# Issuing all engines' instructions straight into the main program instead of into a block with branches and a closing barrier

## The chip, the cores and the metric

The kernel runs on one core of a Trainium2 chip. The profile has records of five engines: TensorE (PE; busy for 246.9 of the 251.6 us of the kernel before), VectorE (DVE; 215.9), ScalarE (ACT; 114.6), GpSimd (POOL; 32.6) and SyncE (SP), whose records are transfers, waits and its share of two barriers, with one branch; none of them counts as busy time. The metric is the device time of one execution in microseconds (us); lower is better. Every run also has a *span*: from the start of the program's first instruction to the end of its last. Time minus span is called "the remainder" below: the part of the measured time that lies outside the program's own instructions. Spans are on record to 0.1 us, so one remainder is good to some 0.05 us. The remainder also holds whatever lies before the first instruction.

## The reference

One layer on 2048 tokens of 640 features in bfloat16. It is cut here to what matters; the change doesn't touch the arithmetic.

```python
x  = A_x                                   # 1 x 2048 x 640
xn = layernorm(x)
q, k, v = split(xn @ wqkv)                 # 32 heads of 20
# each token looks at itself and at 7 earlier ones, 2 apart
o  = softmax(q . k[window] * 20 ** -0.5) @ v[window]
g, u = xn @ w_gate, xn @ w_up              # 1536 features each
return x + o @ wo + (g * u) @ w_down
```

## The kernel before

A small scheduler records every operation with its dependences, and then writes one list of instructions and waits per engine. This is how the lists become a program:

```python
    def emit(self, finals):
        ...                                   # (cut: which waits each instruction needs)
        for X in finals:                      # finals: the nine stores of the output
            prog["sp"].append((0,) + X.event)
        clock = self.clock

        def make_section(ename):
            def section(eng):
                for it in prog[ename]:
                    if it[0] == 0:
                        eng.wait_ge(it[1], it[2])
                        continue
                    ...                       # (cut: issue the instruction, attach its semaphore)
            return section

        with nc.Block() as block:
            block.sync(make_section("sp"))
            block.scalar(make_section("act"))
            block.tensor(make_section("pe"))
            block.vector(make_section("dve"))
            block.gpsimd(make_section("pool"))
```

The block gives each engine a piece of program of its own: a branch into it at the start, a branch out of it at the end (ten as written; the trace has only one of them, see step 2 at the end), and then a barrier of all five engines (in the trace of before five DRAINs and six semaphore instructions at L208, of which the last ends at 251.55 us). An opening barrier, ahead of the block, belongs to the main program and is there with or without the block (it releases the engines from some 0.66 us on). SyncE's list ends with waits for the stores.

The last token tile is stored in three parts; in the profile of before the last matmul ends at 249.26 us by the trace, and the last store, of 32 KB, is issued at 249.62:

```python
            if last:
                eng = "act" if c0 == DHALF else "sp"
                stores.append(dma(ohbm[t * TS:(t + 1) * TS, cols], o, r=[o], name=f"odma{t}_{c0}", eng=eng))
```

Of the kernel before, what the change touches and what calls it, by code (L numbers as in the profile page):

```python
# [41 lines left out]
class Sched:  # L42
# [115 lines left out]
    def emit(self, finals):  # L158
        nc = self.nc
        counters = {e: 0 for e in ENGINES}  # L160
        for X in self.ops:
            if not X.dma and X.needs_tick:
                counters[X.eng] += 1
                X.event = (self.clock[X.eng], counters[X.eng])
        know = {e: {} for e in ENGINES}
        prog = {e: [] for e in ENGINES}
        for X in self.ops:
            E = X.eng
            kn = know[E]
            needed = {}  # L170
            for d in X.deps:
                sem, val = d.event
                if kn.get(sem, 0) >= val:
                    continue
                cur = needed.get(sem)
                if cur is None or cur[0] < val:
                    needed[sem] = (val, d)
            for sem, (val, d) in sorted(needed.items(), key=lambda t: -t[1][1].idx):
                if kn.get(sem, 0) >= val:
                    continue  # L180
                prog[E].append((0, sem, val))
                for s2, v2 in d.pre_know.items():
                    if kn.get(s2, 0) < v2:
                        kn[s2] = v2
                kn[sem] = max(kn.get(sem, 0), val)
            X.pre_know = dict(kn)
            prog[E].append((1, X))
        for X in finals:
# [9 lines that stand above are left out]
                    X = it[1]  # L198
                    ins = X.fn(eng)
                    if ins is not None and X.name:  # L200
                        ins.annotate(X.name)
                    if X.dma:
                        ins.then_inc(X.event[0], 16)
                    elif X.needs_tick:
                        ins.then_inc(clock[ename], 1)
            return section

        with nc.Block() as block:  # L208
            block.sync(make_section("sp"))
            block.scalar(make_section("act"))  # L210
            block.tensor(make_section("pe"))
            block.vector(make_section("dve"))
            block.gpsimd(make_section("pool"))


def build_kernel(nc, A_x, A_wqkv, A_wo, B_x, B_w_gate, B_w_up, B_w_down, out):
# [773 lines left out]
```

## Time and profile before

| What | Before |
|---|---|
| median of the first three runs | 253.53 us (253.51 to 253.69) |
| profiled run: time, span, remainder | 253.35, 251.6, 1.75 us |
| TensorE busy | 246.9 us, 98% of the span |
| first recorded 512-wide matmul of the back-to-back stretch starts | 18.21 us |
| last store is issued | 249.62 us |
| from there to the end of the span | 1.93 us |

The prediction shows the page's lines and the instructions of the closing barrier. This one is the timeline of TensorE of the kernel before, where the long back-to-back stretch begins; columns: start in us, duration in us, engine, line, operation, output and inputs.

```profile
18.21 0.38 PE L479 MATMUL PS<-XNT,WQKV 128*128 128x512 bf16 x1
```

From here to 249.30 us TensorE is busy for 230.05 of 231.09 us, and the chain that ended last holds nothing but its matmuls over that stretch, with gaps of at most 0.05 us: there the time is that of the matmuls. Ahead of it stands the start of the kernel, where loads and layer norms alternate.

### The profile page before, as it was taken

Reading aid. Unit: us, or ns where it says so; the run is one execution under the profiler, and the core shown is the slowest. Engines: PE = TensorE matmul, PEld = TensorE weight load, DVE = VectorE, ACT = ScalarE, POOL = GpSimd, SP = SyncE. Lnnn points to the kernel's source line nnn. Section 1 sums busy time; section 2 is a strip of 40 time slices with the busy share of each in tenths; the row PEclk is TensorE's granted clock in tenths of the full one; section 3 lists DMA queues with packets and bytes.
Section 4 is the critical chain, followed back from the end, with each engine's and each line's share of the span. In section 5 each row is a group of like instructions: output and inputs, shape, how many; then the busy total and the mean of one; then the engine's idle time right before and its main releaser. Section 6 shows DMA issues by size and latency. Waiting matters only on the chain.

```text
span 251.6 us, 3257 instructions
## 1 busy us (share of the span) xinstructions
PE 246.9 (98%) x1274; PEld 128.9 (51%) x1294; DVE 215.9 (86%) x255; ACT 114.6 (46%) x203; POOL 32.6 (13%) x41
## 2 busy tenths in 40 slices
PE   8999999999999999999999999999999999999996
PEld 3995555555544444444444444444444444445775
DVE  4899889999999953999999994899999999995221
ACT  5486657555555557555555553225555011111000
POOL 1000001044434231002331100002000000200200
PEclk9999999999999999999999999999999999999999
DMA  6999879674678462355369932296500011581651
GB/s 181 318 268 211 111 211 406 153 123 87 126 146 136 75 125 42 143 195 104 63 128 269 491 111 42 42 337 57 89 0 3 21 42 21 78 112 23 95 136 52
DMA packets 33775, 33.78 MB, mean 134 GB/s; under 512 B 17984, under 2 KB 30272, under 8 KB 33728
## 3 DMA queue, kind: packets, MB, share of 16 engines
q1 hardware_dynamic: 27280, 24.13, 33.6%
q0 software_dynamic: 6192, 9.31, 22.7%
q8 instruction: 10, 0.16, 0.3%
q10 hardware_dynamic: 288, 0.13, 0.2%
q14 instruction: 5, 0.04, 0.0%
HBM read 14.42 MB, written 4.59 MB: 76 GB/s over the span
## 4 chain that ended last, share of the span: by engine, by line
PE 91%; DVE 3%; SPq 2%; DMA 2%; issue 1%; ACT 0%
PE PS L642 41%; PE PS L669 22%; PE PS L479 21%; PE PS L701 7%; SPq L298 2%; DMA XST<-in_A_x_dram 2%; DVE STATS L376 1%; DVE STATS L382 1%; DVE MV L388 0%; DVE XNS L423 0%; ACT SD L389 0%; DVE FOUT L705 0%; DVE SD L408 0%
## 5 line engine op out<-in xcount | busy, mean ns | idle before, releaser
L642 PE MATMUL PS<-XNT,WU 128*128 128x512 bf16 x237 | 59.0, 379 | 0.2
L642 PE MATMUL PS<-XNT,WG 128*128 128x512 bf16 x232 | 57.9, 379 | 0.4
L479 PE MATMUL PS<-XNT,WQKV 128*128 128x512 bf16 x245 | 53.7, 379 | 0.3
L609 DVE TENSOR_TENSOR PVB<-VO,ATB 128x10240 f16<-128x10240 bf16 x8 | 43.9, 5488 | 0.2
L479 PEld LDWEIGHTS PS<-XNT,WQKV 128*128 128x128 bf16 x250 | 29.4, 118 | 24.4
L644 ACT ACTIVATE USX<-PS 128x512 bf16<-128x512 f32 x48 | 28.7, 597 | 22.6 <-PE PS L642 22.6
L642 PEld LDWEIGHTS PS<-XNT,WU 128*128 128x128 bf16 x240 | 23.5, 98 | 28.3
L642 PEld LDWEIGHTS PS<-XNT,WG 128*128 128x128 bf16 x240 | 23.5, 98 | 28.3
L604 DVE TENSOR_TENSOR PVB<-PVB 128x5120 f16<-128x5120 f16 (+1 forms) x16 | 34.5, 2154 | 0.3
L537 POOL DMA_DIRECT2D LOG<-PE x24 | 21.9, 925 | 58.3 <-DMA LOG<-PE 58.3
L644 ACT ACTIVATE HT<-PS 128x512 bf16<-128x512 f32 x36 | 21.5, 597 | 16.4 <-PE PS L642 16.4
L675 ACT ACTIVATE DT<-PS 128x512 f16<-128x512 f32 x15 | 8.9, 596 | 42.6 <-PE PS L669 39.5
L669 PE MATMUL PS<-HT,WD 128*128 128x512 bf16 x118 | 27.4, 379 | 0.1
L526 DVE TENSOR_TENSOR TMP<-QH,KH 128x2048 f16<-128x2048 bf16 x16 | 19.1, 1217 | 1.0 <-ACT KH L486 0.9
L669 PEld LDWEIGHTS PS<-HT,WD 128*128 128x128 bf16 x120 | 11.7, 98 | 14.2
L526 DVE TENSOR_TENSOR PP<-QH,KH 128x2048 f16<-128x2048 bf16 x16 | 18.9, 1217 | 0.0
L531 DVE TENSOR_TENSOR PP<-PP,TMP 128x4096 f16<-128x4096 f16 x8 | 18.3, 2291 | 0.2
L669 PE MATMUL PS<-VO,WO 128*128 128x512 bf16 x74 | 18.4, 379 | 0.0
L705 DVE TENSOR_TENSOR FOUT<-PS,XR 128x320 bf16<-128x320 f32 (+2 forms) x9 | 4.1, 454 | 15.3 <-PE PS L701 15.3
L537 POOL DMA_DIRECT2D PE<-PP x8 | 8.3, 1043 | 63.1 <-DVE PP L532 63.1
L486 ACT ACTIVATE VO<-PS 128x512 bf16<-128x512 f32 x20 | 11.9, 597 | 8.7 <-PE PS L479 8.7
L647 DVE TENSOR_TENSOR HT<-HT,USX 128x512 bf16<-128x512 bf16 x36 | 14.3, 415 | 1.7 <-ACT USX L644 1.7
(71 smaller groups left out, 220.7 us busy)
## 6 DMA issues: line engine op xcount, KB each, us to landing
PE<-PP POOLq DMA_DIRECT2D x8, 512.0 KB, 4.8
ATB<-LOG SPq DMA_DIRECT2D x8, 512.0 KB, 4.9
LOG<-PE POOLq DMA_DIRECT2D x24, 128.0 KB, 2.7
WG<-in_B_w_gate_dram SPq DMA_DIRECT2D x1, 1920.0 KB, 8.0
WU<-in_B_w_up_dram SPq DMA_DIRECT2D x1, 1920.0 KB, 14.6
WD<-in_B_w_down_dram SPq DMA_DIRECT2D x1, 1920.0 KB, 10.0
out_dram<-in_A_x_dram SPq DMA_DIRECT2D x1, 1920.0 KB, 10.5
out_dram<-FACC POOLq DMA_DIRECT2D x3, 640.0 KB, 6.7
```

Of the source, the lines that this page charges most:

```text
L479: op("pe", (lambda l, x, c: lambda e: e.matmul(PS[:, b, :], l, x, start=(c == 0), stop=(c == NCH - 1)))(l, x, c), r=[l, x], w=[PS[:, b, :] ...
L486: op("act", lambda e: e.activation(o, PS[:, b, :], ACT.Copy, scale=sc), r=[PS[:, b, :]], w=[o], name=f"pev{which}_{m}_{j}")
L526: return (1.22, lambda: op("dve", lambda e: e.tensor_tensor(o, qw, kw, ALU.mult), r=[q, k], w=[o], name=f"prod{h}_{p}_{c}"))
L531: (2.3, lambda: op("dve", lambda e: e.tensor_tensor(a, a, b, ALU.add), r=[a, b], w=[a], name=f"psum{h}_{p}")),
L537: op("pool", lambda e: e.dma_start(o, i, accum_op=ALU.add), r=[o, i], w=[o], dma=True, name=name)
L604: return lambda: op("dve", lambda e: e.tensor_tensor(o, x, y, ALU.add), r=[x, y], w=[o], name=f"{name}_{b}")
L609: lambda: op("dve", lambda e: e.tensor_tensor(PVB[:], vw, aw, ALU.mult), r=[v, a], w=[PVB[:]], name=f"pv_{b}")),
L642: op("pe", (lambda l, x, c: lambda e: e.matmul(PS[:, b, :], l, x, start=(c == 0), stop=(c == NCH - 1)))(l, x, c), r=[l, x], w=[PS[:, b, :] ...
L644: op("act", lambda e: e.activation(o, PS[:, b, :], ACT.Copy), r=[PS[:, b, :]], w=[o], name=f"guev{which}_{m}_{j}")
L647: h_pending.append(lambda: op("dve", lambda e: e.tensor_tensor(h, h, o, ALU.mult), r=[h, o], w=[h], name=f"h{m}_{j}"))
L669: op("pe", (lambda l, x, i: lambda e: e.matmul(PS[:, b, :], l, x, start=(i == 0), stop=(i == n - 1)))(l, x, i), r=[l, x], w=[PS[:, b, :]], ...
L701: op("pe", (lambda l, x, i, b, wid: lambda e: e.matmul(PS[:, b, 0:wid], l, x, start=(i == 0), stop=(i == n - 1)))(l, x, i, b, wid), r=[l, ...
```

## The change

The intent: drop what the block adds around the work, which is ten branches and the closing barrier, and let SyncE's waits for the stores be the last thing in the program.

```diff
-        with nc.Block() as block:
-            block.sync(make_section("sp"))
-            block.scalar(make_section("act"))
-            block.tensor(make_section("pe"))
-            block.vector(make_section("dve"))
-            block.gpsimd(make_section("pool"))
+        for ename, eng in (("sp", nc.sync), ("act", nc.scalar), ("pe", nc.tensor), ("dve", nc.vector), ("pool", nc.gpsimd)):
+            make_section(ename)(eng)
```

The file becomes four lines shorter there, so line L298 becomes L294.

## The prediction

> **What bounds the kernel now.** I read the page first: the span, the busy shares, the forty slices and the chain that ended last.
>
> ```profile
> span 251.6 us, 3257 instructions
> PE 246.9 (98%) x1274; PEld 128.9 (51%) x1294; DVE 215.9 (86%) x255; ACT 114.6 (46%) x203; POOL 32.6 (13%) x41
> PE   8999999999999999999999999999999999999996
> ...
> PE 91%; DVE 3%; SPq 2%; DMA 2%; issue 1%; ACT 0%
> ```
>
> TensorE is busy in every slice, at full granted clock, and the chain is TensorE for 91% of the span. The change touches no matmul, load, store or wait between engines in the middle. Compared instruction by instruction, each engine's stream is the same in both programs, in the same order, except at its start and at its end. So two places of the profile matter: the first microsecond and the last two. Next I read the timeline from 248.5 us on:
>
> ```profile
> 248.74 0.35 ACTq L298 DMA_DIRECT2D out_dram<-FOUT  x1
> ...
> 249.30 0.29 DVE L705 TENSOR_TENSOR FOUT<-PS,XR 128x128 bf16<-128x128 f32 x1 [0.59 <-PE PS L701]
> 249.62 0.33 SPq L298 DMA_DIRECT2D out_dram<-FOUT  x1
> ```
>
> The last arithmetic ends at 249.30 + 0.29 = 249.59 us. SyncE then issues the last store, of 32 KB, and the page's list of issues gives such a store 1.5 us to landing: 249.62 + 1.5 = 251.12 us. The rest is the program's ending. I asked for the instructions of the line that opens the block (L208; its closing barrier is put down to it) and of the helper's wait (L196):
>
> ```profile
> L208 POOLq EVENT_SEMAPHORE  x2: 17/17/17, 251.4 to 251.4; - x2
> L208 POOLq DRAIN  x1: 7977/7977/7977, 234.0 to 234.0; - x1
> L208 PEldq DRAIN  x1: 1222/1222/1222, 248.1 to 248.1; - x1
> L208 ACTq DRAIN  x1: 152/152/152, 249.1 to 249.1; - x1
> L208 DVEq DRAIN  x1: 330/330/330, 249.3 to 249.3; - x1
> L208 SPq COMPARE_BRANCH  x1: 41/41/41, 251.2 to 251.2; - x1
> L208 SPq DRAIN  x1: 13/13/13, 251.3 to 251.3; - x1
> L208 SPq EVENT_SEMAPHORE  x1: 17/17/17, 251.5 to 251.5; - x1
> L208 ACTq EVENT_SEMAPHORE  x1: 17/17/17, 251.5 to 251.5; - x1
> L208 DVEq EVENT_SEMAPHORE  x1: 21/21/21, 251.5 to 251.5; - x1
> L208 PEldq EVENT_SEMAPHORE  x1: 51/51/51, 251.5 to 251.5; - x1
> ```
>
> ```profile
> L196 SPq EVENT_SEMAPHORE  x4: 28/28/28, 250.0 to 251.1; - x4
> ```
>
> Columns: line, engine ("q" is its sequencer), operation, count, shortest/median/longest duration in ns, first and last start in us. The reader is to see that the long DRAINs (GpSimd 7977 ns, TensorE 1222 ns) began early and were over by about 242 and 249.3 us, beside work that had to be done anyway. Only SyncE's last wait, its branch and the hand-shake after it come one after another, past the last store.
>
> [...] the barrier's instructions are 13 to 51 ns each, while the stretch that they fill is some 0.4 us, so I work with start times and not with durations. [...] the one branch in this trace has 41 ns as its duration, and the next instruction of its engine starts some 0.15 us after the branch does. [...] the profiled run took 253.35 us for a span of 251.6, so 1.75 us lie outside the program. [...] the opening barrier releases the engines at about 0.7 us, and SyncE, ScalarE and VectorE start between 0.74 and 0.82 us.
>
> **The change, part by part.**
>
> 1. *The opening barrier stays.* It is put down to the last line of the program (L975), not to the block, and its instructions are in both programs. Nothing is gained there: 0.
>
> 2. *The five branches into the block go.* The block's sections were lines L209 to L213; the trace has no instruction at any of these lines, though the program as built has five branches there. Either they were never executed[...] or they weren't recorded. I chose the first, for this reason: in stretches of 0.02 us, SyncE's release from the opening barrier ends by 0.68 us, and its first load is issued at 0.74 us, a gap of at most 0.08 us; the branch that was recorded at the end took 0.15 us up to the next instruction, which doesn't fit. Of the five branches out of the block too, only SyncE's is in the trace, and that is the one which carries a wait (for one of the stores)[...]. Expected: 0, at most 0.08 us.
>
> 3. *SyncE's branch at the end goes, and its wait moves.* Before, nine waits for stores sat on four wait instructions, two each, and one on the branch. After, they sit on five wait instructions (1 + 2 + 2 + 2 + 2). The last of the five waits for the same last store as the fourth did before. The additional one, 28 ns, comes first, when stores that landed long ago are asked for; it lies in the 1.5 us in which SyncE waits for the last store anyway. Added on the path: 0.
>
> 4. *The closing barrier goes* (five DRAINs and six semaphore instructions). From the same fine stretches: the last store wait executes at 251.09 us and ends 28 ns later, at 251.12; the branch is seen from 251.16; SyncE's DRAIN at 251.32; GpSimd's two semaphore instructions at 251.36 and 251.44; the releases of the others from 251.48, and TensorE's, the last, ends at about 251.56, which the page rounds to 251.6. After the change the program's last instruction is the store wait, ending at 251.12. Removed from the path: 251.56 - 251.12 = 0.44 us, of which about 0.20 us is the branch with its gaps (251.12 to 251.32) and 0.24 us the hand-shake SyncE to GpSimd to all.
>
> Sum: span 251.56 - 0.44 = 251.1 us. If the 1.75 us outside it stay, the time becomes 253.53 - 0.44 = 253.09 us, a ratio of 0.9983. I put 253.05[...].
>
> **The rivals.**
>
> [...] the 0.44 us shrinks to 0 to 0.2. [...] Against: all DRAINs but SyncE's 13 ns one were over by 249.6 us, 1.5 us ahead of the end. It would give 253.3 to 253.5 us, with a shorter span and a larger remainder outside.
>
> *More than the span's share comes back.* [...] If part of the 1.75 us is work that each engine does for itself [...], this part becomes hidden for four engines. SyncE remains last and still has its own share, which speaks against a large gain. It would give 252.5 to 252.9 us.
>
> *The middle shifts.* [...] The chain from 18 to 249 us is TensorE back to back, which lets small shifts of loads do nothing; and the three runs of before span only 0.18 us (253.51 to 253.69). It would give plus or minus 0.1 us. For a change over 2% either way 5.1 us would be needed, more than twelve times what the whole closing stretch holds, and no view has idle time of that size which a branch or barrier ends. [...] the instruction queues moved only 0.20 MB at 0.3% of the DMA time.
>
> **Range and chances.** I give the plain sum, with the outside unchanged, some 65%: 252.9 to 253.25 with the scatter. [...] a further gain 15%. The range of 252.75 to 253.4 leaves out the far ends of both rivals. Within 2%: 0.985; faster by over 2%: 0.01; slower by over 2%: 0.005.
>
> **What would show it right or wrong.** Right: a span near 251.1 us; no DRAIN and no GpSimd semaphore instruction after the last store; SyncE with one more store wait, the last of them starting about 1.5 us after the last store's issue and being the final record; no COMPARE_BRANCH; some 3246 instructions (3257 minus eleven of the barrier and one branch, plus one wait), give or take missing matmul records; SyncE's first load still near 0.74 us. Step 2 falls if the first load is issued by 0.65 us or earlier while the opening barrier hasn't moved. Step 4 falls if the span shortens by 0.4 us and the time doesn't, which is the first rival, or if the time falls by over 0.7 us, which is the second. The whole falls if TensorE's stretch from 18 us to the last matmul has another length than before by more than 0.2 us.

The sum came to 253.53 - 0.44 = 253.09 us and was put down as 253.05: the 0.04 us between them was an estimate; nothing measured stood behind it. Of the rivals, the first, with 20% of the chances, is that the 0.44 us are paid again outside the span; the case for it was not shown by anything. The second is that a part of the 1.75 us runs earlier when an engine ends earlier: with the block the last records of all five engines end at 251.47 to 251.55 us, and without it four of them were to end between 242 and 249.6 us. How the middle could shift, in the third, was a guess.

## The result

| | Before | After |
|---|---|---|
| median of six runs | 253.66 us (253.51 to 254.37) | 252.57 us (252.28 to 253.00) |
| ratio | | 0.9956 (95% interval 0.9940 to 0.9971) |
| profiled run: time, span, remainder | 253.35, 251.6, 1.75 us | 252.93, 251.6, 1.33 us |

A ratio is the mean time of one kernel's fast runs over the mean of the other's in the same rounds, so it is not quite the ratio of the medians. The interval is clear of 1: the change is a gain of 1.1 us in these runs, where 0.5 was forecast, and the median lies 0.18 us below the range.

The page of the kernel after:

```profile
span 251.6 us, 3246 instructions
PE 247.3 (98%) x1274; PEld 129.3 (51%) x1294; DVE 215.8 (86%) x255; ACT 114.6 (46%) x203; POOL 32.6 (13%) x41
...
PE 96%; DVE 1%; ACT 1%; DMA 1%; issue 1%
```

Eleven instructions fewer, as forecast, and busy times within 0.4 us. But the span of the profiled run isn't shorter at all. Two readings resolve this. The first is the timeline of TensorE at the place that was shown for before:

```profile
18.71 0.38 PE L475 MATMUL PS<-XNT,WQKV 128*128 128x512 bf16 x1 [0.23 <-issue]
```

In this run the back-to-back stretch began 0.50 us later than in the profiled run of before. (Both traces lack 20 of the 1294 matmul records, the very first of the stretch among them, so both starts are about 0.22 us too late; their difference stands.) The second is the end of the timeline of the kernel after, and the helper's waits (columns of the second: line, engine, operation, count, shortest/median/longest duration in ns, first and last start in us):

```profile
249.81 0.29 DVE L701 TENSOR_TENSOR FOUT<-PS,XR 128x128 bf16<-128x128 f32 x1 [0.59 <-PE PS L697]
250.13 0.33 SPq L294 DMA_DIRECT2D out_dram<-FOUT  x1
```

```profile
L196 SPq EVENT_SEMAPHORE  x5: 17/28/28, 250.5 to 251.6; - x5
```

The last store is issued at 250.13 us, and the fifth wait, the last record of the program, ends at 251.63 by the trace: 1.50 us. Before it was 1.93 us. So the ending inside the span did shrink, by 0.43 us, and a late start hid it in this one run. Meanwhile the other engines had left: their last recorded instructions end at 235.83 (GpSimd), 249.61 (ScalarE), 249.77 (TensorE) and 250.10 us (VectorE), at least 1.5 us ahead of SyncE's (251.63).

Does the change delay the start? The first load is issued at 0.741 us in the trace of before and at 0.745 in that of after, and from the first 512-wide matmul to the last store's issue the traces have 231.416 and 231.414 us (231.630 to 231.637 in the twelve later profiles, which have all matmul records). Over all fourteen profiles the stretch began anywhere from 17.84 to 18.90 us, with programs whose recorded instructions there are the same. In the two controls below it began at 18.11 (before) and 18.15 us (after). It is scatter of the start, whose cause wasn't looked for, and its full range is larger than what the change does. That the first three runs of before looked so much alike (0.18 us from end to end) was chance: later ones range from 253.01 to 254.38 us.

The spans for the six runs of the changed kernel are 251.6, 251.1, 251.0, 251.1, 251.4 and 251.7 us: they scatter, but the remainders are 1.28 to 1.33 us in all six. The one run of before with a span on record had 1.75. So a second gain, of nearly 0.5 us, appears where no instruction of the program is: outside the span. (The traces have the spans to 1 ns: 251.554 and 251.629 us, so that the two remainders are 1.80 and 1.30.) The experiments are about that one.

### The profile page after: what moved, and what is told of

The parts are those of the page before. It is cut to its first block, busy times and chain, and to the rows that moved or that the text cites. A ratio compares the mean times of both kernels' runs of the same rounds, so it can differ in the third digit from the quotient of the medians.

```text
span 251.6 us, 3246 instructions
## 1 busy us (share of the span) xinstructions
PE 247.3 (98%) x1274; PEld 129.3 (51%) x1294; DVE 215.8 (86%) x255; ACT 114.6 (46%) x203; POOL 32.6 (13%) x41
## 4 chain that ended last, share of the span: by engine, by line
PE 96%; DVE 1%; ACT 1%; DMA 1%; issue 1%
PE PS L638 41%; PE PS L665 22%; PE PS L475 21%; PE PS L697 7%; PE PS L499 2%; PE PS L773 1%; PE PS L492 1%; DMA XST<-in_A_x_dram 1%; ACT XNS L394 0%; PE PS L434 0%; ACT XNS L392 0%; DVE XNS L419 0%; DVE STATS L372 0%; DVE STATS L378 0%; ACT SD L397 0%
```

## The experiments

Theory of early arrival: what lies outside the span is supposed to hold a part for each engine, which can begin once that engine has left, that is, has come to the end of its own instructions. With the block, all five engines leave together, after SyncE's last wait (251.5 us in the profile of before). Without it, four of them leave early (by 250.10 us in that of after), and their parts would run while SyncE still waits (to 251.63 us). No trace has an instruction there; the theory is supposition, to be tried by the remainders alone. The rivals: the barrier's own instructions, or the branches, cost something that shows only outside the span. And within the theory: does one engine account for it, or does every late engine add a step?

Twelve kernels were run (two of them the kernels before and after, as controls), in three sets, each set on one chip with runs of the kernel before beside it. The remainders, with their means over all timed runs:

| Run | Who leaves after the last store has landed | Runs | Mean time, us | Mean span, us | Mean remainder (range), us | Ratio to before |
|---|---|---|---|---|---|---|
| c_before | all five, from the barrier | 5 | 253.51 | 251.72 | 1.79 (1.76 to 1.83) | 0.9998 |
| c_after | SyncE | 5 | 252.76 | 251.48 | 1.28 (1.25 to 1.31) | 0.9968 |
| e_barrier | all five, from a barrier without a block | 6 | 253.58 | 251.78 | 1.80 (1.76 to 1.83) | 1.0002 |
| e_all_wait | all five, no barrier | 5 | 252.89 | 251.10 | 1.79 (1.76 to 1.82) | 0.9973 |
| e_pe_wait | SyncE, TensorE | 3 | 252.79 | 251.27 | 1.52 (1.51 to 1.54) | 0.9977 |
| e_act_wait | SyncE, ScalarE | 3 | 252.66 | 251.23 | 1.42 (1.40 to 1.45) | 0.9971 |
| e_dve_wait | SyncE, VectorE | 3 | 252.76 | 251.37 | 1.40 (1.36 to 1.46) | 0.9976 |
| e_pool_wait | SyncE, GpSimd | 3 | 253.03 | 251.23 | 1.80 (1.78 to 1.82) | 0.9986 |
| e_pool_early | SyncE; GpSimd 0.8 us earlier | 3 | 252.63 | 251.37 | 1.27 (1.25 to 1.29) | 0.9961 |
| e_act_last | ScalarE | 3 | 252.61 | 251.13 | 1.47 (1.46 to 1.48) | 0.9960 |
| e_dve_last | VectorE | 3 | 252.83 | 251.40 | 1.43 (1.42 to 1.44) | 0.9969 |
| e_pool_last | GpSimd | 3 | 253.45 | 251.63 | 1.82 (1.78 to 1.86) | 0.9994 |

The remainder is the sharp instrument here: it repeats within 0.1 us for a kernel, while times and spans carry the scatter of the start (the spans of the 26 runs of before reach from 251.2 to 252.6 us). A ratio of this table that rests on three runs has an interval of 0.5 to 0.8 us to either side and can't rank two kernels that are 0.1 us apart.

### c_before and c_after: the controls

No edit. First the kernel before:

> Control: the kernel before, unchanged, run as an experiment so that the span of every run is on record. The question is how much of the time lies outside the span. The one profiled run had 253.35 - 251.6 = 1.75 us there; the six runs of the changed kernel have 1.28 to 1.33. If the remainder is a property of the kernel, all runs here have 1.70 to 1.80 outside, and the spans scatter by some 0.5 us as those of the changed kernel did (251.0 to 251.7). If it is a property of one run, the remainder scatters too. Ratio 1.000.

Then the kernel after:

> Control: the changed kernel, unchanged, again. Expected as its six runs on record: median near 252.6, spans 251.0 to 251.7, 1.28 to 1.33 us outside, ratio 0.9956 within 0.0015. Against the control of before, the mean span should be shorter by the 0.44 us of the closing stretch; if it is shorter by much more or less, the difference lies in the first 18 us [...].

The remainder belongs to the kernel, not to a run: with the runs of before that stood beside the three sets, 26 runs of before have 1.74 to 1.83 us (mean 1.79), and eleven of after have 1.25 to 1.33 (mean 1.30). That is 0.49 us. The two profiles happen to have starts within 0.04 us of each other, so they can be laid side by side. The last store's issue in the timeline, c_before first and then c_after:

```profile
249.74 0.33 SPq L298 DMA_DIRECT2D out_dram<-FOUT  x1
```

```profile
249.78 0.33 SPq L294 DMA_DIRECT2D out_dram<-FOUT  x1
```

By the trace the two programs end at 251.67 and 251.28 us: 1.93 and 1.50 us after these issues, the same values as in the first two profiles. The second control's ratio is 0.9968 (0.9953 to 0.9983), its mean 0.76 us below that of the first (the mean spans differ by 0.24 us, where 0.44 was expected); on the first rounds the gain was 1.1 us. Both are the 0.43 + 0.49 = 0.92 us of the change with the scatter of the start on top, once against it and once for it: over all 26 and eleven runs with spans the means are 253.56 and 252.69 us, 0.88 us apart. Of this the spans have 0.39, against 0.43 us of the ending, so on average the start of the two kernels is the same within some 0.04 us.

### e_barrier: the barrier alone, without branches

```diff
             make_section(ename)(eng)
+        nc.all_engine_barrier()
```

> The changed kernel with the closing barrier alone put back at its end, without any branch. Theory of early arrival [...]: all five leave together, so the remainder outside goes back to 1.75 us; the span regains the hand-shake, 0.24 us, but not the branch with its gaps, 0.20; time some 0.7 us above the changed kernel, ratio to before 0.999. Rival, the branches cost what lies outside [...]: the remainder stays at 1.31 and the time is 0.24 us above the changed kernel, ratio 0.9965.

The remainder is back at 1.80 us, so it isn't the branches that cost outside the span. The barrier's instructions in this profile, with the issue of the last store from its timeline:

```profile
249.75 0.33 SPq L295 DMA_DIRECT2D out_dram<-FOUT  x1
```

```profile
L210 POOLq EVENT_SEMAPHORE  x2: 17/17/17, 251.3 to 251.4; - x2
...
L210 SPq DRAIN  x1: 13/13/13, 251.3 to 251.3; - x1
L210 SPq EVENT_SEMAPHORE  x1: 17/17/17, 251.4 to 251.4; - x1
L210 ACTq EVENT_SEMAPHORE  x1: 17/17/17, 251.4 to 251.4; - x1
L210 DVEq EVENT_SEMAPHORE  x1: 21/21/21, 251.4 to 251.4; - x1
L210 PEldq EVENT_SEMAPHORE  x1: 51/51/51, 251.5 to 251.5; - x1
```

SyncE's DRAIN now starts 0.04 us after the end of its last wait; in the first profile of before a COMPARE_BRANCH stood between the two (wait to 251.12 us, branch at 251.160, DRAIN at 251.333). The program ends at 251.50 by the trace, 1.75 us after the store's issue. Between 1.93 and 1.75 lies the branch with its gaps, 0.18 us; between 1.75 and 1.50 lies the hand-shake, 0.25 us. The time, 0.8 us above c_after, was to be 0.7 above.

### e_all_wait: late, but without a barrier

```diff
             make_section(ename)(eng)
+        for eng in (nc.scalar, nc.tensor, nc.vector, nc.gpsimd):
+            eng.wait_ge(*finals[-1].event)
```

> The changed kernel with one wait more at the end of each of the four other engines: for the landing of the last store, as SyncE waits. No barrier, no hand-shake, no branch; only the lateness of the four engines comes back. Theory of early arrival: span as the changed kernel within 0.05 us (TensorE's wait is some 0.03 longer), remainder 1.75 us, time 0.44 us above the changed kernel, ratio to before 0.9973. Rival, the barrier's own instructions (drains, GpSimd's semaphore steps) cost what lies outside: remainder 1.31 us, time and ratio as the changed kernel.

The remainder is 1.79 us with no drain, no hand-shake and no branch. What sets this kernel apart from the changed one are these four waits alone:

```profile
L211 ACTq EVENT_SEMAPHORE  x1: 17/17/17, 250.9 to 250.9; - x1
L211 POOLq EVENT_SEMAPHORE  x1: 17/17/17, 250.9 to 250.9; - x1
L211 DVEq EVENT_SEMAPHORE  x1: 21/21/21, 250.9 to 250.9; - x1
L211 PEldq EVENT_SEMAPHORE  x1: 51/51/51, 250.9 to 250.9; - x1
```

They are 17 to 51 ns long, all within SyncE's last wait but for TensorE's, which ends 0.03 us after it, and yet they cost 0.5 us outside the span. That is the lateness itself. The rival, that the barrier's instructions cost what lies outside, falls. (The mean time is only 0.13 us above c_after, because the starts of these five runs fell early: the profiled one began its long stretch at 17.84 us, the earliest. That the ratio is the expected 0.9973 is luck for the same reason.)

### e_pe_wait, e_act_wait, e_dve_wait, e_pool_wait: one late engine at a time

The edit, here for TensorE; the others have `nc.scalar`, `nc.vector` and `nc.gpsimd` in its place:

```diff
             make_section(ename)(eng)
+        nc.tensor.wait_ge(*finals[-1].event)
```

TensorE:

> The changed kernel, and TensorE alone of the four other engines waits for the last store too. So far: 1.28 us outside the span when SyncE leaves last, alone; 1.79 when all five leave together. Theory A, one slow engine: what lies outside is the longest of the engines' own shares, and one engine alone brings back the whole 0.5 us, the other three nothing. Theory B, a chain of steps from engine to engine: each late engine delays the chain from its own place on, so that the engine which comes first in the chain brings back the whole 0.5 us, and the later ones less and less, in steps. TensorE has the longest wait instruction, 51 ns, so I hold it the likeliest slow one: 1.79 under A; between 1.28 and 1.79 under B.

ScalarE:

> The changed kernel, and ScalarE alone waits for the last store too. Theory A (one slow engine, probably TensorE or GpSimd): 1.28 us outside, as the changed kernel. Theory B (a chain from engine to engine): a value of its own between 1.28 and 1.79.

VectorE:

> The changed kernel, and VectorE alone waits for the last store too. Theory A: 1.28 us outside. Theory B: a value of its own between 1.28 and 1.79, different from ScalarE's by a step.

GpSimd:

> The changed kernel, and GpSimd alone waits for the last store too. Theory A: 1.79 us if GpSimd is the slow engine (its drain is the longest of the five in the profile), else 1.28. Theory B: a value of its own between the two.

(In the profile of before GpSimd's DRAIN takes 7977 ns, the next longest, TensorE's, 1222.)

GpSimd alone brings back all of it: 1.80 us, as much as all five together. TensorE, which I held to be the likeliest, brings 1.52, ScalarE 1.42 and VectorE 1.40; SyncE has 1.28. These don't add up (the excesses over 1.28 sum to 1.02 us, and all engines together have 0.51), as it would be if the engine with the largest figure decided. Theory A as I had put it, one slow engine and nothing from the others, is too simple, since each engine has a figure of its own. Theory B, a chain with a place for each engine, gives the same order of figures. The runs don't tell the two apart, nor do they show either at work; what can be fitted to them is a rule: the end is the latest, over the engines, of an engine's own leaving plus its own figure. Checked with the spans of the traces, by which GpSimd's figure is 1.83 us (see the last experiments), the rule gives 1.79 us for e_all_wait, where the profiled run has 1.80. It gives a little too little where there is a barrier: in c_before and e_barrier GpSimd's last instruction ends 0.087 us before the span does, so the rule says 1.74 us, and the profiled runs have 1.79 and 1.80. What adds these 0.05 us is open.

### e_pool_early: late by how much

```diff
             make_section(ename)(eng)
+        nc.gpsimd.wait_ge(*finals[-2].event)
```

> The changed kernel, and GpSimd alone waits too, but for the store before the last (ScalarE's, of 192 columns), which SyncE sees landed some 0.8 us before the last one. With the wait for the last store GpSimd brought 1.80 us outside, SyncE alone 1.28, so GpSimd's own share seems 0.52 us longer. If it is a matter of when it leaves, a lead of 0.8 us covers the 0.52 and the remainder is 1.28 us, as the changed kernel. Rival: a wait instruction at GpSimd's end costs by being there, whenever it is met: 1.80 us.

GpSimd's wait instruction is there in both kernels, and only the moment differs. In e_pool_wait, where the last store was issued at 250.06 us:

```profile
L210 POOLq EVENT_SEMAPHORE  x1: 17/17/17, 251.5 to 251.5; - x1
```

In e_pool_early, where it was issued at 249.96 us by the trace:

```profile
L210 POOLq EVENT_SEMAPHORE  x1: 17/17/17, 250.7 to 250.7; - x1
```

With a lead of some 0.8 us the remainder is 1.27 us, as without the wait. So GpSimd could leave that late for free here. By the rule above it has to cover the difference of the two figures, 0.52 us for GpSimd; that is an estimate from them, since no lead between 0 and 0.8 us was tried. GpSimd's wait instruction, 17 ns, costs nothing by being there: 1.27 us, beside 1.28 in c_after.

### e_act_last, e_dve_last, e_pool_last: another engine as the last

```diff
-            prog["sp"].append((0,) + X.event)
+            prog["act"].append((0,) + X.event)
```

(and `"dve"` or `"pool"` likewise). ScalarE:

> The changed kernel with the nine waits for the stores at ScalarE's end in place of SyncE's; SyncE leaves after its last issue. ScalarE and SyncE together had 1.42 us outside. If each engine has a share of its own and the longest counts, ScalarE alone has 1.42. If there is a chain and SyncE's place in it adds, it is less, down to 1.28 or below; below 1.28 it would beat the changed kernel. Span as the changed kernel but for the scatter at the start (251.0 to 251.8).

VectorE:

> The same with the nine waits at VectorE's end. VectorE and SyncE together had 1.40 us outside. Longest share: 1.40. A chain to which SyncE adds: less, and below 1.28 it would beat the changed kernel.

GpSimd:

> The same with the nine waits at GpSimd's end, the engine that alone brought back the whole difference. Longest share: 1.80 us outside, and a time as long as that of the kernel with all five engines waiting, some 0.5 us above the changed kernel. If GpSimd costs only because SyncE is late as well, less than 1.80.

The figures are those of the pairs, within 0.05 us: 1.47, 1.43 and 1.82. SyncE's own share added nothing to them. With the spans of the traces, which aren't rounded to 0.1 us, the agreement is closer still: the profiled runs have 1.45 us in both kernels for ScalarE, 1.39 in both for VectorE and 1.83 in both for GpSimd, beside 1.56 for TensorE in its pair and 1.29 to 1.31 where SyncE decides (after, c_after, e_pool_early). So ScalarE's figure and VectorE's, whose ranges in the table of pairs overlap, do differ. None of the three is cheaper as the last one than SyncE with 1.28 us, so there is no version here that beats the changed kernel; TensorE as the only last one wasn't run. The median of e_act_last, 252.58 us, is level with the changed kernel's only through the start (mean span 251.13 against 251.39); by its remainder it is 0.17 us worse than the eleven runs' 1.30. With GpSimd last the gain outside the span is gone, and with late starts (the profiled run began its long stretch at 18.90 us) the time is that of the kernel before: 0.9994 (0.9961 to 1.0027).

## Why the prediction was wrong

**The range was missed through one term of the sum: the one outside the span.** The step that failed reads "If the 1.75 us outside it stay". They don't stay: 1.79 us become 1.30. The prediction had this as its second rival ("this part becomes hidden for four engines"), and gave it 15%, because "SyncE remains last and still has its own share, which speaks against a large gain". This sentence takes all shares to be alike. They aren't: SyncE's is 1.28 us, the smallest of the five, and GpSimd's 1.80 us, the largest. Leaving SyncE last and alone was worth the whole difference. The allowance of 0.04 us (253.09 put down as 253.05, by an estimate) should have been about 0.5: 253.53 - 0.44 - 0.49 = 252.60. That this is so near the measured 252.57 is partly luck: the six runs of before had a median of 253.66, from which the sum gives 252.73, and the other 0.16 us is scatter of the start. The prediction's own sign for the second rival, a time lower by over 0.7 us, did appear; only, step 4, which it was to overturn, held beside it. Nothing in the profile of before could give the shares, but the 1.75 us were in plain sight, and a part of such a size of which nothing is known deserved a wider range downwards.

Point by point:

- *Step 1, the opening barrier stays: right.* It has the same instructions in both profiles.
- *Step 2, the entry branches cost 0 to 0.08 us: right.* The first load moved from 0.741 to 0.745 us. That the nine other branches were never executed was an inference from their absence in the trace, and was not shown beyond that: the trace of before has a single COMPARE_BRANCH, SyncE's at 251.160 us, and that of after none.
- *Step 3, SyncE's additional wait is free: right.* There are five waits, and the new one, which asks for one store and not two, takes 17 ns, not 28; it starts at 250.5 us, and the last of the five at 251.6.
- *Step 4, 0.44 us off the closing stretch: right.* It was 0.43 us in both pairs of profiles; of this the branch has 0.18 (forecast 0.20) and the hand-shake 0.25 (forecast 0.24). That split was shown by e_barrier.
- *A span near 251.1 us: missed in the profiled run (251.6), about right on average.* The eleven runs of after have a mean span of 251.39 us and the 26 of before 251.78, 0.39 apart. The start scatters by 1 us, which three runs that happened to lie within 0.18 us of each other had hidden; "the chain from 18 to 249 us" was indeed immovable, and the scatter all lies ahead of it.
- *First rival, the 0.44 us are paid again outside the span: wrong.* The remainder shrank, from 1.79 to 1.30 us, instead of growing.
- *Third rival, the middle shifts: wrong.* 231.416 against 231.414 us, and 231.630 in both controls.
- *Two slips of arithmetic or reading, without effect.* 5.1 us are 11.6 times the 0.44 us of the closing stretch, not "more than twelve"; and SyncE's DRAIN starts 0.173 us after its branch does (251.160 to 251.333 us by the trace), not 0.15.
- *Chances:* within 2% had 0.985, and that is how it came out.

What the time outside the span consists of isn't shown by any run, since the trace has no instruction there. What the runs show is its length: 1.28 us when SyncE alone leaves last, 1.79 us when all five engines leave together.

## What to carry to other kernels

The barrier at the end of this program cost more than its own instructions (0.25 us inside the span): with it every engine left late, and 1.79 us lay outside the span, as much as with GpSimd alone late (1.80 us), where it was 1.28 with SyncE alone: 0.5 us. Let each engine leave as soon as its work is done, and let the engine with the smallest remainder, SyncE here with 1.28 us, hold the last wait; GpSimd's leaving 0.8 us ahead of it was free here (1.27 us), and by the estimate above some 0.5 us would do. Subtract the span from the time before anything else, look at it over many runs, and don't read a difference of spans from one profile when the start of the kernel scatters by more than the effect.
